# A fused chunk-attention and gated-MLP kernel on one core: the first w_in piece cast in halves, the last w_out piece and the h3 loads exchanged, the last block's small loads begun a block later

## The chip, the cores and the metric

One core of one Trainium2 chip. The metric is the device time of one execution in microseconds. Before the change: 295.74 us, median of 3 runs (294.94 to 296.02). A timed execution lasts about 1.7 us longer than the span that the profile of the same execution shows, from the first to the last instruction. The execution that was profiled for this "before" took 296.49 us, 0.75 more than the median.

## The reference

```python
# q, k, v: 8 x 8 x 576 x 64, float32; softmax attention inside chunks of 64
scores = (1 / sqrt(64)) * q_c @ k_c.transpose(0, 1, 2, 4, 3)
attn = exp(scores - max); attn = attn / (sum(attn) + 1e-9)
x = (attn @ v_c).transpose(...).reshape(4608, 512)
h = x @ w_in                                  # 512 x 2048
g = h * (1 / (1 + exp(-beta * h)))
out = g @ w_out                               # 2048 x 512
```

The kernel works on 9 blocks of 512 rows of x. Block n has two halves of attention, h = 2n and 2n + 1, so "h5" is the second half of block 2. For each half come, in order: loads of k, q, v; casts to bf16 (POOL); a transpose of q and k (for h2 to h5 on DVE, from h6 by DMA followed by an ordering copy on POOL); scores (PE); exp (ACT); averages (PE); normalising to xn (DVE); a transpose of xn to xT (on PE at first, from block 3 by DMA). Then mm1 (x by w_in, 64 matmuls per block), the gate g (ACT and DVE) and mm2 (g by w_out, 64 matmuls).

## The kernel before

The program declares operations with a rank, and a small scheduler in the kernel file turns them into **one fixed, in-order queue per engine** before the kernel is built. A change of one rank or load can therefore move instructions on several engines. These are the parts that the change touches:

```python
def cast_w_in(j, c0, c1, eng):                 # piece j of w_in, 512 columns
    s, f0, n = PIECES[j]
    stage, names = stage_w_in(j)
    cast(eng, n * (c1 - c0), w_in_bf[:, c0:c1, f0:f0 + n], stage[:, c0:c1, :],
         keys(names, ("in", j)), [K("w_in", j, c) for c in range(c0, c1)])
...
ORDER = (("w", 0), ("w", 1), ("h", 2), ("w", 2))   # loads after w_in: w_out pieces, halves
LATER = (("h", 3), ("w", 3))
...
def load_half(h, after=None):
    load(load_qk, h, 1, "sp", after=after)         # k, then q, then v in two parts
    first = load(load_qk, h, 0, "sp", after=after)
    for cp in range(2):
        load(load_v, h, cp, "sp", after=after)
    return first
...
for j in range(4):
    for c, eng in enumerate(("pool", "act", "pool", "dve" if j else "act")):
        go(0, cast_w_in, j, c, c + 1, eng)
...
for h in (2, 3):
    attention(h)
load_half(4)
load_half(5)
...
for blk in range(2, NB):                           # cut
    for i in range(16):
        go(r, mm1, blk, i, n)
        done = gated[blk, i] = go(0, gate, blk, i, n)
        if 2 <= blk < 7:                           # 24 small loads of the last block
            for fn, args, kw in small[3 * (16 * (blk - 2) + i) // 10:3 * (16 * (blk - 2) + i + 1) // 10]:
                go(5000, fn, *args, "sp", after=done, **kw)
        go(r + 2, mm2, blk - 1, s, range(p, p + w), m)
```

The softmax here doesn't subtract the row's maximum and nothing guards it: scores larger than these inputs give would overflow.

Of the kernel before, what the change touches and what calls it, by code (L numbers as in the profile page):

```python
# [12 lines left out]
def K(*key, v=0):  # L13

    return key, v
# [276 lines left out]
def bass_chunk_attention__then__act_swish_beta_kernel(nc, q, k, v, w_in, w_out, beta, out):  # L292
# [7 lines left out]
    with ExitStack() as es:  # L300
        def sb(name, shape, t):
            return es.enter_context(nc.sbuf_tensor(name, shape, t))

        P = Program(nc, es, 64)
# [4 lines left out]
        w_in_bf = sb("w_in_bf", [128, NC, DFF], BF16)  # L309
# [20 lines left out]
        A0, A1, A2, A3, F3, F0, F1, F2 = range(8)  # L330
        FS = (F0, F1, F2, F3)

        def bank(n):
            return A[:, n, :]

        def act_us(n):
            return 0.186 + 0.833e-3 * n
# [4 lines left out]
        def pool_us(n):  # L342
            return 0.07 + 1.02e-3 * n

        def copy(eng, us, dst, src, reads, writes, **kw):
            if eng == "act":
                P.op("act", us, lambda e: e.activation(dst, src, AF.Copy, **kw), reads, writes)  # L347
            else:
                P.op(eng, us, lambda e: e.tensor_copy(dst, src), reads, writes)  # L349

        def cast(eng, n, *args):
            us = {"act": act_us(n), "dve": 0.12 + 0.56e-3 * n, "pool": pool_us(n)}[eng]
            copy(eng, us, *args)
# [40 lines left out]
        def keys(names, v):  # L394
            return [K(*n, v=v) for n in names]
# [48 lines left out]
        def stage_w_in(j):  # L444
            s, f0, n = PIECES[j]
            return wstage[:, s, :].rearrange("p (c f) -> p c f", c=4), \
                [("wst", s, x, c, hb) for x in range(2) for c in range(4) for hb in range(2)]
# [5 lines left out]
                stage, w_in[:, f0:f0 + n].rearrange("(c p) f -> p c f", p=128)),  # L453
                writes=keys(names, ("in", j)))

        def cast_w_in(j, c0, c1, eng):
            s, f0, n = PIECES[j]
            stage, names = stage_w_in(j)
            cast(eng, n * (c1 - c0), w_in_bf[:, c0:c1, f0:f0 + n], stage[:, c0:c1, :],
                 keys(names, ("in", j)), [K("w_in", j, c) for c in range(c0, c1)])  # L460

        def stage_w_out(j):
            if j < 2:
# [225 lines left out]
        def piece_of(t):  # L689
            return t // 4  # L690

        def mm1(blk, t, n, halves=(0, 1)):
            sx = blk % 2
            m, j = divmod(t, 2)
            hs, c = slice(halves[0], halves[-1] + 1), slice(256 * halves[0], 256 * halves[-1] + 256)
            for kt in range(4):
                def f(e, kt=kt):
                    u, y = divmod(kt, 2)
                    return e.matmul(  # L699
                        bank(n)[:, c].rearrange("p (x t) -> p x t", t=64),  # L700
                        w_in_bf[:, kt, 256 * m:256 * m + 256].rearrange("p (x t) -> p t x", t=2)[:, j, :],
                        xT[:, sx, hs, :, :, u, 64 * y:64 * y + 64].rearrange("p v k c t -> p (v k c) t"),
                        start=(kt == 0), stop=(kt == 3))
                P.op("pe", 0.108 * len(halves), f, reads=[K("w_in", piece_of(t), kt)]
                     + [K("xT", sx, hv, y, v=2 * blk + hv) for hv in halves for y in range(2)],
                     writes=[K("ps", n, v=("h", blk, t))])

# [51 lines left out]
        def go(rank, fn, *args, slack=0, line=False, after=None, **kw):  # L759
            P.call += 1  # L760
            P.rank, P.slack, P.line, P.after, P.name = rank, slack, line, after, (fn.__name__,) + args
            fn(*args, **kw)
            P.after = None
            return P.ops[-1]
# [2 lines left out]
        FIRST = 10  # L767
        TURNED, XTURNED = 6, 6
        SL = 1.5
        TD = {2: -2, 3: 0}  # L770
        ALONE = (4, 5)
        go(-9, make_identity)
        go(-9, make_ones)
        loads = [0]
        gated = {}
        ORDER = (("w", 0), ("w", 1), ("h", 2), ("w", 2))
        LATER = (("h", 3), ("w", 3))
        URGE = {1: -1, 4: 2, 5: 2}
        TA, TB = -4, 4

        def load(fn, *args, after=None):
            loads[0] += 1
            return go(loads[0], fn, *args, line=after is None, after=after)

        def load_half(h, after=None):
            load(load_qk, h, 1, "sp", after=after)
            first = load(load_qk, h, 0, "sp", after=after)
            for cp in range(2):
                load(load_v, h, cp, "sp", after=after)
            return first  # L790

        def rank_of(h):
            return -1000 + 10 * h

        def turn(h, banks=None):
            r = rank_of(h)
            for w in (1, 0):
                if h >= 2:
                    go(r, cast_rows, h, w, "pool")
                    for hb in range(2):  # L800
                        go(TD.get(h, 2), turn_dve, h, w, hb)
                    continue
                for j in range(2):
                    go(URGE.get(h, 0), cast_qk, h, w, j, 4, ("dve", "act")[j] if h == 0 else ("dve", "pool")[j])
                for j in range(2):
                    go(r, turn_pe, h, w, j, 4, banks[2 * w + j])
                for j in range(2):
                    go(URGE.get(h, 0), keep_turned, h, w, j, 4, banks[2 * w + j],
                       "act" if h == 1 and w == 0 else ("dve", "act")[j])
            for cp in range(2):  # L810
                go(r + 1, cast_v, h, cp, "pool")

        def score(h, sb=A0):
            go(rank_of(h), *((scores, h, (0, 1), sb) if h < 2 else (scores_halved, h)))
            for cp in range(2):
                go(URGE.get(h, 0), *((exp, h, (cp,), sb) if h < 2 else (exp_halved, h, cp)))

        def average(h, banks=(A2, A0)):
            r = rank_of(h)
# [9 lines left out]
        def group(h):  # L829
            x = waiting.pop(0) if waiting and (h is None or waiting[0] <= h - 2) else None  # L830
            go(-3, turn_group, h, x, slack=0.7)

        def attention(h):
# [4 lines left out]
            else:  # L838
# [7 lines left out]
                if h < FIRST + 1:  # L846
                    go(r, scores, h, (0, 1), slack=SL)
                else:
                    go(r, attend_and_score, h - 1, slack=SL)
                    go(0, normalize_all, h - 1)  # L850
# [4 lines left out]
            elif h < FIRST:  # L855
                go(r, attend, h, (0, 1), slack=SL)
                for cp in range(2):
# [5 lines left out]
        first = load_half(0)  # L863
# [13 lines left out]
        score(1, F0)  # L877
        average(1)
        for what in ORDER:
            load(load_w_out, what[1], "sp") if what[0] == "w" else load_half(what[1])  # L880
        go(0, turn_beta, F2)
        for i in range(NWARM[2]):
            go(1e6, warm, F3, 64)
        for j in range(4):
            for c, eng in enumerate(("pool", "act", "pool", "dve" if j else "act")):
                go(0, cast_w_in, j, c, c + 1, eng)
        for t in range(4):
            go(10 * t, mm1, 0, t, FS[t], (0,))
# [6 lines left out]
        for j in range(3):  # L895
            for i in range(4):
                go(0, cast_w_out, j, i, ("pool", "dve")[i % 2])
        for what in LATER:
            load(load_w_out, what[1], "sp") if what[0] == "w" else load_half(what[1])
        for i in range(4):  # L900
            go(0, cast_w_out, 3, i, ("pool", "dve")[i % 2])
        for h in (2, 3):
# [27 lines left out]
        small = []  # L930
# [3 lines left out]
        for blk in range(2, NB):  # L934
            if blk < LAST:
                for h in (2 * blk + 2, 2 * blk + 3):
                    if blk + 1 < LAST:
                        load_half(h, after=gated[divmod(16 * (blk - 1) + (TA, TB)[h % 2], 16)])
                    attention(h)
            else:  # L940
                while waiting:
                    group(None)
                go(-500, attend_all, 2 * LAST + 1, slack=SL)
                go(0, normalize_all, 2 * LAST + 1)
                waiting.append(2 * LAST + 1)
                group(None)
            for i in range(16):
                n = FS[i % 2]
                r = 100 * blk + 400 + 4 * i
                go(r, mm1, blk, i, n)  # L950
                done = gated[blk, i] = go(0, gate, blk, i, n)
                if 2 <= blk < 7:
                    for fn, args, kw in small[3 * (16 * (blk - 2) + i) // 10:3 * (16 * (blk - 2) + i + 1) // 10]:
                        go(5000, fn, *args, "sp", after=done, **kw)
                w = 4
                s, p = divmod(w * i, 16)
                m = FS[2 + s % 2] if 2 * blk + 2 < FIRST else F2
                go(r + 2, mm2, blk - 1, s, range(p, p + w), m)
                if p + w == 16:
                    finish(blk - 1, s, m)  # L960
# [4 lines left out]
        for j in range(2):  # L965
            cols, n = (256 * j, 256 * j + 256), (F3, F0)[j]
# [56 lines left out]
```

## Time and profile before

| | before |
|---|---|
| timed | 295.74 us (3 runs) |
| span of the profiled execution | 294.8 us |
| PE busy | 280.0 us (95%) |
| DVE, ACT, POOL busy | 147.8, 147.8, 114.8 us |

PE is the bound, so the useful view is the list of what PE waited for. These are its rows of the kernel before that lie after the first 20 us; the columns are the releaser, the total in us, the number of times, the longest:

```profile
PE A L699 <- issue: 1.5, 1, 1.5
PE A L563 <- POOL qkO L349: 0.9, 1, 0.9
PE A L583 <- DVE xT L349: 0.5, 1, 0.5
PE A L699 <- DVE g L717: 0.2, 1, 0.2
```

L699 is mm1, L563 and L583 are scores. In order of time they stand at 47.6 (0.5), 57.8 (0.2, behind the gates g of block 1), 79.7 (0.9) and 105.3 us (1.5, block 3's first mm1). The last of these places is **block 3's start at about 104**.

### The profile page before, as it was taken

How to read it: one execution, taken by the hardware profiler on the slowest of the kernel's cores; microseconds unless marked ns; L12 is line 12 of the kernel's file. 1: busy time of each engine (PE TensorE's matmuls, PEld its weight loads, DVE VectorE, ACT ScalarE, POOL GpSimd, SP SyncE). 2: the span in 40 equal slices, each digit the busy share in tenths (PEclk: the TensorE clock that was granted, in tenths of full speed). 3: DMA queues.
4: the chain of work that ended last, by engine and by line, in shares of the span. 5: the costliest groups of instructions: out<-in, count | busy, mean ns of one | idle time of the engine just before them, and what ended most of it. 6: DMA issues, size and time to landing. Idle time of an engine off the chain costs nothing.

```text
span 294.8 us, 6064 instructions
## 1 busy us (share of the span) xinstructions
PE 280.0 (95%) x2584; PEld 137.6 (47%) x2584; DVE 147.8 (50%) x268; ACT 147.8 (50%) x224; POOL 114.8 (39%) x117
## 2 busy tenths in 40 slices
PE   2879998999899979999999999999999999999995
PEld 2655444644444434444444444444444444444444
DVE  2547967897356435436363636363635544334300
ACT  4548713675546525545455555555545445454311
POOL 1534655535776564554545657504350000000000
PEclk9989999999999999999999999999999999999999
DMA  7999999999989999999999898828282310101133
GB/s 202 307 389 400 285 334 313 316 260 242 217 221 205 212 284 188 295 177 254 176 271 185 262 204 227 128 89 143 91 127 98 64 71 0 73 0 71 51 88 77
DMA packets 91722, 55.97 MB, mean 190 GB/s; under 512 B 76712, under 2 KB 76976, under 8 KB 91696
## 3 DMA queue, kind: packets, MB, share of 16 engines
q1 hardware_dynamic: 91520, 55.46, 76.0%
q8 instruction: 20, 0.33, 0.4%
q10 hardware_dynamic: 176, 0.14, 0.2%
q14 instruction: 6, 0.05, 0.1%
HBM read 36.71 MB, written 9.44 MB: 157 GB/s over the span
## 4 chain that ended last, share of the span: by engine, by line
PE 81%; DMA 10%; SPq 3%; DVE 2%; POOL 2%; issue 1%; POOLq 0%
PE A L727 40%; PE A L699 38%; DMA wstage<-in_moe_w_in_dram 3%; DMA qkT<-qkb 3%; SPq L417 2%; DMA qkstage<-in_k_dram 2%; DMA qkstage<-in_q_dram 2%; PE A L612 2%; PE A L563 1%; POOL qkO L349 1%; DVE g L717 1%; SPq L432 1%; DVE qkO L521 0%; POOL w_in_bf L349 0%; DVE w_out_bf L349 0%
## 5 line engine op out<-in xcount | busy, mean ns | idle before, releaser
L717 DVE SCALAR_TENSOR_TENSOR g<-tt,A 128x512 bf16<-128x512 bf16 x144 | 97.7, 685 | 99.5 <-ACT tt L714 98.4
L699 PE MATMUL A<-xT,w_in_bf 128*128 128x512 bf16 (+1 forms) x608 | 142.1, 371 | 2.9 <-issue 1.5
L714 ACT ACTIVATE tt<-A,beta_half 128x512 bf16<-128x512 f32 x144 | 98.1, 688 | 90.2 <-PE A L699 89.9
L727 PE MATMUL A<-w_out_bf,g 128*128 128x512 bf16 (+1 forms) x592 | 140.0, 374 | 0.2
L699 PEld LDWEIGHTS A<-xT,w_in_bf 128*128 128x128 bf16 x608 | 57.9, 99 | 66.4 <-DVE g L717 6.1
L727 PEld LDWEIGHTS A<-w_out_bf,g 128*128 128x128 bf16 x592 | 56.6, 98 | 65.0 <-POOL w_out_bf L349 0.8
L349 POOL COPY qkO<-qkT 128x1024 bf16<-128x1024 bf16 x24 | 47.2, 1977 | 36.3 <-DMA qkT<-qkb 36.3
L349 POOL CAST qkb<-qkstage 128x1024 bf16<-128x1024 f32 (+1 forms) x30 | 30.7, 1025 | 23.8 <-DMA qkstage<-in_k_dram 12.7
L347 ACT ACTIVATE ostage<-A 128x512 f32<-128x512 f32 (+1 forms) x36 | 21.3, 591 | 17.6 <-PE A L727 17.6
L652 DVE TENSOR_TENSOR xn<-A,R 128x512 bf16<-128x512 f32 (+2 forms) x44 | 25.4, 592 | 1.2
L349 POOL CAST v_bf<-vstage 128x512 bf16<-128x512 f32 x32 | 19.7, 616 | 16.2 <-DMA vstage<-in_v_dram 15.8
L600 ACT ACTIVATE E<-A 128x1024 bf16<-128x1024 f32 (+1 forms) x16 | 14.4, 915 | 10.3 <-PE A L612 8.1
L657 DVE RECIPROCAL R<-A 128x8 f32<-128x8 f32 (+2 forms) x36 | 7.2, 199 | 12.5 <-PE A L612 12.5
L521 DVE STREAM_TRANSPOSE qkO<-qkb 128x256 uint32<-128x256 uint32 x16 | 9.3, 650 | 4.0 <-POOL qkb L349 4.0
L612 PEld LDWEIGHTS A<-v_bf,E 64*64 64x64 bf16 x576 | 6.9, 107 | 7.1 <-issue 4.2
L612 PE MATMUL A<-v_bf,E 64*64 64x65 bf16 x576 | 9.8, 195 | 0.0
L502 PE MATMUL A<-ident,qkb 128*128 128x128 bf16 x32 | 3.5, 267 | 6.4 <-DVE qkb L349 6.3
L592 ACT ACTIVATE E<-A 128x512 bf16<-128x512 f32 x8 | 4.5, 596 | 8.0 <-PE A L583 8.0
L349 POOL CAST w_in_bf<-wstage 128x512 bf16<-128x512 f32 x8 | 4.9, 640 | 7.8 <-DMA wstage<-in_moe_w_in_dram 7.8
L349 POOL CAST qkb<-wstage 128x1024 bf16<-128x1024 f32 x4 | 4.2, 1043 | 9.5 <-issue 9.5
L563 PE MATMUL A<-qkO 64*64 64x64 bf16 x448 | 6.6, 198 | 0.9 <-POOL qkO L349 0.9
L741 DVE TENSOR_SCALAR ostage<-A 128x256 f32<-128x256 f32 x1 | 0.4, 425 | 13.3 <-PE A L727 13.3
(35 smaller groups left out, 65.1 us busy)
## 6 DMA issues: line engine op xcount, KB each, us to landing
qkstage<-in_k_dram SPq DMA_DIRECT2D x16, 512.0 KB, 5.1
qkstage<-in_q_dram SPq DMA_DIRECT2D x16, 512.0 KB, 5.6
vstage<-in_v_dram SPq DMA_DIRECT2D x32, 256.0 KB, 6.4
out_dram<-ostage SPq DMA_DIRECT2D x16, 512.0 KB, 4.1
wstage<-in_moe_w_in_dram SPq DMA_DIRECT2D x4, 1024.0 KB, 9.9
qkstage<-in_moe_w_out_dram SPq DMA_DIRECT2D x2, 1024.0 KB, 14.8
g<-in_moe_w_out_dram SPq DMA_DIRECT2D x2, 1024.0 KB, 8.9
wstage<-in_q_dram SPq DMA_DIRECT2D x8, 128.0 KB
```

The costliest lines, as they stand in the source:

```text
L347: P.op("act", us, lambda e: e.activation(dst, src, AF.Copy, **kw), reads, writes)
L349: P.op(eng, us, lambda e: e.tensor_copy(dst, src), reads, writes)
L521: P.op("dve", 0.1 + 2.05e-3 * 256, lambda e: e.transpose(dst, qkb[:, s, which, 4 * hb:4 * hb + 4, :].rearrange("p a x -> p (a x)").bitcast ...
L563: return e.matmul(bank(b + hb)[64 * c2:64 * c2 + 64, 64 * i:64 * i + 64], qkO[r, s, 1, hp, 64 * c:64 * c + 64], qkO[r, s, 0, hp, 64 * c:64 ...
L600: P.op("act", act_us(128 * (b - a)), lambda e: e.activation(E[:, s, :, a:b, :].rearrange("p g i q -> p g (i q)"), S[:, :, 64 * a:64 * b], ...
L612: return e.matmul(bank(n)[64 * y:64 * y + 64, 65 * j:65 * j + 65], E[r, s, hb, 4 * cp + hp, :], v_bf[r, sv, 2 * hv + cp, 2 * hp + hb, 0:65])
L652: P.op("dve", 0.15 + 1.05e-3 * n, lambda e: e.tensor_tensor(dst, o[..., 0:64], r.unsqueeze(len(r.shape)).to_broadcast(shape), ALU.mult), r ...
L657: P.op("dve", 0.22, lambda e: e.reciprocal(r, o[..., 64]), reads=[K("ps", b, v=("o", h)) for b in banks], writes=[K("R", banks[0], v=h)])
L699: return e.matmul(bank(n)[:, c].rearrange("p (x t) -> p x t", t=64), w_in_bf[:, kt, 256 * m:256 * m + 256].rearrange("p (x t) -> p t x", t ...
L714: P.op("act", 0.075 + act_us(N), lambda e: e.activation(tt[:, T % 3, c], bank(n)[:, c], AF.Tanh, scale=beta_half[:, t:t + 1]), reads=[K("p ...
L717: P.op("dve", dve_us(N), lambda e: e.scalar_tensor_tensor(g2[:, sg, t, c], tt[:, T % 3, c], 1.0, bank(n)[:, c], ALU.add, ALU.mult), reads= ...
L727: P.op("pe", 0.2158 * (b - a) / 512, lambda e, t=t: e.matmul(bank(n)[:, 0:b - a], g2[:, sg, t, rows], w_out_bf[:, t, a:b], start=(t == 0), ...
```

## The change

Three parts. (1) The first w_in piece is cast in eight half casts on POOL, ACT and DVE, so that mm1 can start on a half. (2) The last two loads of the LATER list change places. The one-line description says "h3 loaded ahead of the last w_out piece"; the code does the reverse: the last w_out piece now goes ahead of h3. (3) The 24 small loads for the last block begin in block 3 instead of block 2. The diff without its settings that change nothing (they spell out what was implicit before); left out, too, is the line in which mm1 now names the half of the w_in piece that it reads:

```diff
-        def cast_w_in(j, c0, c1, eng):
+        def cast_w_in(j, c0, c1, eng, xs=(0, 1)):
...
+            a, b = 256 * xs[0], 256 * xs[-1] + 256
+            cast(eng, (b - a) * (c1 - c0), w_in_bf[:, c0:c1, f0 + a:f0 + b], stage[:, c0:c1, a:b],
+                 keys(names, ("in", j)), [K("w_in", j, c, x) for c in range(c0, c1) for x in xs])
...
+        SMALL = 3
+        FIRST_CASTS = (("pool", "act", "dve", "pool"), ("act", "pool", "act", "pool"))
...
-        LATER = (("h", 3), ("w", 3))
+        LATER = (("w", 3), ("qv", 3))
...
-        for j in range(4):
-            for c, eng in enumerate(("pool", "act", "pool", "dve" if j else "act")):
+        for x in range(2):
+            for c, eng in enumerate(FIRST_CASTS[x]):
+                go(-3, cast_w_in, 0, c, c + 1, eng, (x,))
+        for j in range(1, 4):
+            for c, eng in enumerate(("pool", "act", "pool", "dve")):
                 go(0, cast_w_in, j, c, c + 1, eng)
...
-                if 2 <= blk < 7:
-                    for fn, args, kw in small[3 * (16 * (blk - 2) + i) // 10:3 * (16 * (blk - 2) + i + 1) // 10]:
+                if SMALL <= blk < 7:
+                    y = 24 / (16 * (7 - SMALL))
+                    for fn, args, kw in small[int(y * (16 * (blk - SMALL) + i)):int(y * (16 * (blk - SMALL) + i + 1))]:
```

More of the change, by code (lines that the diff above doesn't have):

```diff
@@ L454, in load_w_in @@
                 writes=keys(names, ("in", j)))
-        def cast_w_in(j, c0, c1, eng):
+        def cast_w_in(j, c0, c1, eng, xs=(0, 1)):
             s, f0, n = PIECES[j]
             stage, names = stage_w_in(j)
-            cast(eng, n * (c1 - c0), w_in_bf[:, c0:c1, f0:f0 + n], stage[:, c0:c1, :],
-                 keys(names, ("in", j)), [K("w_in", j, c) for c in range(c0, c1)])
+            a, b = 256 * xs[0], 256 * xs[-1] + 256
+            cast(eng, (b - a) * (c1 - c0), w_in_bf[:, c0:c1, f0 + a:f0 + b], stage[:, c0:c1, a:b],
+                 keys(names, ("in", j)), [K("w_in", j, c, x) for c in range(c0, c1) for x in xs])
         def stage_w_out(j):
@@ L703, in f @@
                         start=(kt == 0), stop=(kt == 3))
-                P.op("pe", 0.108 * len(halves), f, reads=[K("w_in", piece_of(t), kt)]
+                P.op("pe", 0.108 * len(halves), f, reads=[K("w_in", piece_of(t), kt, t // 2 % 2)]
                      + [K("xT", sx, hv, y, v=2 * blk + hv) for hv in halves for y in range(2)],
@@ L769, in bass_chunk_attention__then__act_swish_beta_kernel @@
         SL = 1.5
+        SMALL = 3
+        FIRST_CASTS = (("pool", "act", "dve", "pool"), ("act", "pool", "act", "pool"))
+        PAIRED = (2, 3, 4, 5)
         TD = {2: -2, 3: 0}
@@ L775, in bass_chunk_attention__then__act_swish_beta_kernel @@
         gated = {}
-        ORDER = (("w", 0), ("w", 1), ("h", 2), ("w", 2))
-        LATER = (("h", 3), ("w", 3))
+        ORDER = (("w", 0), ("w", 1), ("qv", 2), ("w", 2))
+        LATER = (("w", 3), ("qv", 3))
         URGE = {1: -1, 4: 2, 5: 2}
@@ L783, in load, with load_half, load_what, turn @@
             return go(loads[0], fn, *args, line=after is None, after=after)
-        def load_half(h, after=None):
-            load(load_qk, h, 1, "sp", after=after)
-            first = load(load_qk, h, 0, "sp", after=after)
-            for cp in range(2):
-                load(load_v, h, cp, "sp", after=after)
-            return first
+        def load_half(h, after=None, parts="qv"):
+            if "q" in parts:
+                load(load_qk, h, 1, "sp", after=after)
+                first = load(load_qk, h, 0, "sp", after=after)
+            if "v" in parts:
+                for cp in range(2):
+                    load(load_v, h, cp, "sp", after=after)
+            return first if "q" in parts else None
+        def load_what(what):
+            if what[0] == "w":
+                load(load_w_out, what[1], "sp")
+            else:
+                load_half(what[1], parts=what[0])
         def rank_of(h):
             return -1000 + 10 * h
-        def turn(h, banks=None):
+        def turn(h, banks=(A0, A1)):
             r = rank_of(h)
             for w in (1, 0):
+                if h >= 2 and h not in PAIRED:
+                    go(r, cast_qk, h, w, 0, 8, "pool")
+                    go(r, turn_pe, h, w, 0, 8, banks[w])
+                    go(URGE.get(h, 0), keep_turned, h, w, 0, 8, banks[w], ("act", "dve")[w])
+                    continue
                 if h >= 2:
@@ L813, in score @@
         def score(h, sb=A0):
-            go(rank_of(h), *((scores, h, (0, 1), sb) if h < 2 else (scores_halved, h)))
+            go(rank_of(h), *((scores_halved, h) if h in PAIRED else (scores, h, (0, 1), sb)))
             for cp in range(2):
-                go(URGE.get(h, 0), *((exp, h, (cp,), sb) if h < 2 else (exp_halved, h, cp)))
+                go(URGE.get(h, 0), *((exp_halved, h, cp) if h in PAIRED else (exp, h, (cp,), sb)))
         def average(h, banks=(A2, A0)):
@@ L879, in bass_chunk_attention__then__act_swish_beta_kernel @@
         for what in ORDER:
-            load(load_w_out, what[1], "sp") if what[0] == "w" else load_half(what[1])
+            load_what(what)
         go(0, turn_beta, F2)
@@ L898, in bass_chunk_attention__then__act_swish_beta_kernel @@
         for what in LATER:
-            load(load_w_out, what[1], "sp") if what[0] == "w" else load_half(what[1])
+            load_what(what)
         for i in range(4):
```

## The prediction

> **What bounds the kernel now.** I read the page first, then the chain that ended last, then the timeline of the places where TensorE (PE) pauses. The page's opening rows:
>
> ```profile
> span 294.8 us, 6064 instructions
> PE 280.0 (95%) x2584; PEld 137.6 (47%) x2584; DVE 147.8 (50%) x268; ACT 147.8 (50%) x224; POOL 114.8 (39%) x117
> PE   2879998999899979999999999999999999999995
> DMA  7999999999989999999999898828282310101133
> ```
>
> PE is the bound: 280.0 of 294.8 us busy, so only 14.8 us of idle exist. The third row says where: the first two slices (7.4 us each), the last one, and digits below 9 around slices 5, 10 and 14. Nothing else on PE changes with this diff: it runs the same 2584 matmuls. The last row says that the DMA engines are full for nearly the first half, which decides below who keeps a gain.
>
> The chain of waits, in order of time, shows what PE hung on in the middle:
>
> ```profile
> 50.01 5.33 DMA qkstage<-in_q_dram
> 55.47 1.05 POOL qkb L349
> ...
> 61.17 5.50 DMA qkstage<-in_k_dram
> 66.67 9.09 DMA qkT<-qkb
> 75.81 3.88 POOL qkO L349 x2
> ...
> 103.80 1.50 issue
> ```
>
> So from 50 to 79.7 us the path runs through loads, a DMA transpose (9.09 us) and two POOL copies, not through PE. PE has work beside it until 78.83 and then waits 0.91 us (row L563 <- POOL qkO). At 103.80 it waits again, 1.50 us. From 105.31 us to the end the chain is PE back to back, so the finish is the moment PE passes 105.31 plus a constant 189.5 us (294.8 - 105.31). This is my main lever: **a saving counts only if it moves that moment.**
>
> The timeline of the two ends of the region:
>
> ```profile
> 18.13 1.15 ACT L347 ACTIVATE w_in_bf<-wstage 128x512 bf16<-128x512 f32 x2 [1.75 <-DMA wstage<-in_moe_w_in_dram]
> 18.16 1.18 POOL L349 CAST w_in_bf<-wstage 128x512 bf16<-128x512 f32 x2 [3.43 <-DMA wstage<-in_moe_w_in_dram]
> 18.83 0.39 PE L699 MATMUL A<-xT,w_in_bf 128*128 128x256 bf16 x2 [0.99 <-POOL w_in_bf L349]
> 19.39 0.91 PE L699 MATMUL A<-xT,w_in_bf 128*128 128x256 bf16 x6 [0.17 <-POOL w_in_bf L349]
> ...
> 95.77 1.57 SPq L423 DMA_DIRECT2D wstage<-in_q_dram  x2
> 97.45 2.75 SPq L539 DMA_TRANSPOSE qkT<-qkb  x2
> 100.25 1.63 SPq L539 DMA_TRANSPOSE xT<-xn  x1
> ...
> 105.31 1.02 PE L699 MATMUL A<-xT,w_in_bf 128*128 128x512 bf16 x4 [1.50 <-issue]
> ```
>
> The upper four: the first w_in piece lands at about 18.13, its four casts run two by two on ACT and POOL until about 19.34, and PE waits for them (0.99 + 0.17 us). The lower four: the xT transpose that block 3's first matmul needs is issued at 100.25. Transposes of xT take 3.1 to 4.9 us (median 4.3) from issue to landing, so 103.4 to 105.2, which fits the matmul's start at 105.31. The "issue" label names no releaser; xT is my reading. Ahead of it in the queue stand two small loads for the last block (1.57 us), and one more at 82.62.
>
> [...] granted clock 0.50 from 20.0 to 23.4, full after; 3.4 us at half rate costs about 1.7 us of matmul time. [...] POOL casts of 512 columns take 616 ns alone and 838 ns where DVE casts at the same moment, whose own time goes from 421 to 631. [...] In this trace the small load at 82.62 held the SP queue 2.6 us for a wait.
>
> **Part 1, casts in halves.** A POOL cast goes from 616 ns to about 0.33 us and an ACT cast from 629 ns to about 0.42 ([...] estimates from these rows); a DVE cast from 421 to about 0.28. Before: first weight ready 18.78, fourth 19.34. After: POOL c0 18.16 to 18.5, ACT c1 to 18.55, DVE c2 [...] to 18.4–18.8, POOL c3 to about 18.85–19.1. The second halves are done at 19.5–19.8. PE starts about 0.3 us earlier, can do 12 matmuls before the last transposes of x instead of 8, and begins the second-half matmuls at about 21.05 instead of 22.2. Of these 16, 11 run at half clock until 23.4 (2.35 us / 0.213) and 5 at full (0.54), ending near 23.95; before, 6 and 10, ending near 24.5. **Gain at this point: 0.55 us.** A cost is hidden in the order: DVE's cast stands between its two normalisations, so the second waits for the landing and xn is ready at 19.3–19.7 instead of 18.22. That meets PE, which only comes to those transposes at about 19.9. [...]
>
> **Part 2, load order.** The description speaks of h3 before the last w_out piece; the code does the reverse. The last w_out piece (1 MB) now goes right behind the third, h3 after it. That piece landed at 47.5 and PE was waiting around it: 0.52 us at 47.12 and the weight loads 0.63 at 49.2. Now it lands near 42.2 (1 MB at about 0.3 MB/us behind 38.8). h3's q lands about 3.5 us later, 45.5 instead of 42.0; cast 1.04 and two DVE transposes 1.3 put its scores at about 47.9–48.2. PE's new order puts 8 more w_out matmuls (8 x 0.216 = 1.73 us) ahead of those scores, so it comes there at 47.12 + 1.73 - 0.55 = 48.3. It just fits. **Gain: the 0.5 us of idle, with up to 0.5 at risk.**
>
> **Together at block 1:** PE is about 1.0 us early at 55. But it then meets the DMA-bound stretch. SP issues without a pause there, and the bytes ahead of h6's q are the same in both kernels. So the qkT landing at 75.76 and PE's restart at 79.74 stay, and the wait of 0.91 grows to about 1.9. **Parts 1 and 2 are given back at 79.7**, except what the altered order of the two output stores moves in the queue: I allow +0.3 us, within -0.5 to +1.
>
> **Part 3, small loads from block 3.** Three of them leave the queue ahead of the xT transpose that is late at 105. SP saves 95.77 to 97.45, 1.65 us. If only the data's time is saved, 2 x 128 KB at 309 GB/s is 0.85 us. So xT lands 0.85 to 1.65 us earlier, 103.6 to 104.4, while PE comes at 103.80 as before. The wait of 1.50 shrinks to between 0 and 0.65: **gain 0.85 to 1.5, middle 1.2.** Later blocks take 6 small loads instead of 4.8, but the running total (6 after block 3 against 9.6, 12 against 14.4, 18 against 19.2, 24 against 24) never exceeds the old one, and PE has no idle there. I charge nothing.
>
> **Sum:** 0 from parts 1 and 2 directly, 0.3 from the altered queue, 1.2 from part 3 = 1.5 us, so 295.74 - 1.5 = 294.2.
>
> **Rivals.** (a) The gains add up, because the DMA stretch moves with PE: 0.55 + 0.5 + 0.9 + 1.5 = 3.4 us, 292.3. For it: the stretch contains gates by DVE g at 57–61, which follow PE. Against it: SP is issuing without a gap until 66.6. (b) The late h3 becomes the new wait at 48, half a microsecond or one. For it: h3's margin is under 0.4 us. Against its mattering: there is 0.9 + 0.55 us of slack before 79.7. It would leave 294.2, and only a slip beyond 1.5 us would show. (c) The xT transpose is late because of the DMA engines (busy share 1.1 to 1.19 from 100 to 106), not the SP queue; then part 3 returns only 0.4 and the time is 295.3. (d) Another order in the queue delays h6 and costs 1 us: 295.5.
>
> **Range and chances.** The middle is 294.2. Rival (a) and an escape from the half clock reach to 292.6, (c) and (d) to 295.5; the old runs alone spread over 1.1 us. I take 292.7 to 295.4. Being 2% faster needs 5.9 us, more than all middle idle and the half clock together (0.55 + 1.35 + 0.5 + 0.9 + 1.5 = 4.8): 3%. Slower by 2% would need a new 6 us stall in a stream of unchanged totals: 1%.
>
> **What would show it.** Right: first w_in matmul near 18.5; the wait near 47 gone; PE's wait before the scores at 79–80 grown to about 1.9 with the restart still near 79.7; the wait near 104 under 0.7; PE solid after that. Wrong: the restart at 79.7 moving earlier with PE (then the sum is too small); a wait of over 1.5 us at h3's scores; the 104 wait unchanged; idle appearing in blocks 3 to 7, where small loads are denser.

The forecast's sum is 0 + 0.3 + 1.2 = 1.5 us, so 294.2. One term outside the sum, a gain of 1.9 us at the head if PE is not at half clock there, stands as 0.55 + 1.35 under "Range and chances", as a possibility for which no trace shows what brings it about. The times of the half casts are estimates; in the look at the change one took 427 ns on POOL, 405 on ACT and 294 on DVE on average, against 616, 629 and 421 for a whole one in the text above.

## The result

295.38 us (median of 6 runs, 294.67 to 296.48) against 295.78 (6 runs, 294.94 to 296.38) of the kernel before beside it. The ratio is 0.999, with a 95% interval of 0.9966 to 1.0015: the same within 2%. Ratios here are the mean time of one kernel's fast runs over the mean of the other's of the same rounds, so not quite the ratio of the medians that are quoted. The forecast was 1.5 us of gain; 0.4 was measured.

The page of the kernel after:

```profile
span 293.7 us, 6073 instructions
PE 278.3 (95%) x2584; PEld 136.7 (47%) x2584; DVE 147.6 (50%) x269; ACT 148.0 (50%) x225; POOL 115.9 (39%) x119
```

What PE waited for after, in the same view as before (L700 is mm1, L584 is scores; every line number has moved by one):

```profile
PE A L700 <- DVE g L718: 2.2, 1, 2.2
PE A L584 <- DVE xT L349: 0.9, 1, 0.9
PE A L700 <- DMA xT<-xn: 0.8, 1, 0.8
```

The wait for POOL at 79.7 is gone, and the wait at block 3 shrank from 1.5 to 0.8. But the wait for the gates at 58 grew from 0.2 to 2.2 us. The head, from the timeline (start, length, engine, operation, and in brackets the idle time before it and its releaser):

```profile
17.99 1.03 ACT L347 ACTIVATE w_in_bf<-wstage 128x256 bf16<-128x256 f32 x3 [1.68 <-DMA wstage<-in_moe_w_in_dram]
17.99 0.29 DVE L349 CAST w_in_bf<-wstage 128x256 bf16<-128x256 f32 x1 [0.67 <-DMA wstage<-in_moe_w_in_dram]
18.02 1.55 POOL L349 CAST w_in_bf<-wstage 128x256 bf16<-128x256 f32 x4 [3.32 <-DMA wstage<-in_moe_w_in_dram]
18.60 1.50 PE L700 MATMUL A<-xT,w_in_bf 128*128 128x256 bf16 x12 [0.82 <-POOL w_in_bf L349]
```

Part 1 works as meant: PE starts at 18.60 and does 12 matmuls at once, where before it did 2 at 18.83 and 6 more at 19.39. In this execution PE also kept its full clock (granted clock 1.00 from 14 to 26 us). It came to h3's scores at 47.43 without a wait, with eight more mm2 matmuls (1.73 us) done than before at 47.64, so 1.9 us early, and to h4's 1.5 early. After 16 more mm1 matmuls it stood still for 2.18 us, until 58.25. Before and after, from PE's timeline:

```profile
55.01 0.71 PE L583 MATMUL A<-qkO 32*64 32x64 bf16 x64
57.78 1.90 PE L699 MATMUL A<-xT,w_in_bf 128*128 128x512 bf16 x8 [0.21 <-DVE g L717]
```

```profile
53.50 0.71 PE L584 MATMUL A<-qkO 32*64 32x64 bf16 x64 [0.85 <-DVE xT L349]
58.25 1.90 PE L700 MATMUL A<-xT,w_in_bf 128*128 128x512 bf16 x8 [2.18 <-DVE g L718]
```

The 0.85 us before h4's scores is a new wait too, for a copy of xT that stands behind two transposes of h4 in DVE's queue. The chain of waits says what the 2.18 us were for (start, length, step):

```profile
48.33 1.05 POOL qkb L349
49.41 1.15 DVE qkO L522 x2
50.61 5.21 DMA qkstage<-in_q_dram
55.94 1.05 POOL qkb L349
58.25 1.90 PE A L700 x8
...
96.51 1.72 SPq L540
98.27 4.86 DMA xT<-xn
103.26 1.89 PE A L700 x8
```

And DVE's timeline just before 58:

```profile
55.70 1.15 DVE L522 STREAM_TRANSPOSE qkO<-qkb 128x256 uint32<-128x256 uint32 x2 [2.25 <-POOL qkb L349]
57.01 0.66 DVE L522 STREAM_TRANSPOSE qkO<-qkb 128x256 uint32<-128x256 uint32 x1 [0.17 <-POOL qkb L349]
57.51 0.68 DVE L718 SCALAR_TENSOR_TENSOR g<-tt,A 128x512 bf16<-128x512 bf16 x1
```

In DVE's in-order queue the first three gates of block 1 stand behind three transposes of h5. Two of these wait for POOL's cast of h5's k, the third for its cast of h5's q, and that waits for h5's q to land. The gates' own inputs, three operations on ACT, were done between 55.5 and 56.6. PE needs the first gate because the gate reads a buffer of A that PE's next matmuls write (so the kernel declares it; the timeline names DVE's g as the releaser of the 2.18 us). So however early PE is, it cannot pass 58 before h5's q has landed (50.61 + 5.21 us), and that load was issued at 50.01 before and 50.61 after.

### The profile page after: what moved, and what is told of

The parts are those of the page before. It is cut to its first block, busy times and chain, and to the rows that moved or that the text cites. A ratio compares the mean times of both kernels' runs of the same rounds, so it can differ in the third digit from the quotient of the medians.

```text
span 293.7 us, 6073 instructions
## 1 busy us (share of the span) xinstructions
PE 278.3 (95%) x2584; PEld 136.7 (47%) x2584; DVE 147.6 (50%) x269; ACT 148.0 (50%) x225; POOL 115.9 (39%) x119
## 4 chain that ended last, share of the span: by engine, by line
PE 77%; DMA 12%; SPq 8%; DVE 1%; POOL 1%; issue 0%; ACT 0%; POOLq 0%
PE A L728 37%; PE A L700 36%; SPq L432 4%; DMA wstage<-in_moe_w_in_dram 3%; DMA qkstage<-in_k_dram 3%; DMA g<-in_moe_w_out_dram 2%; PE A L613 2%; DMA qkstage<-in_q_dram 2%; SPq L417 2%; DMA xT<-xn 2%; PE A L564 1%; SPq L473 1%; SPq L540 1%; POOL qkb L349 1%; DVE qkO L522 1%
## 5 line engine op out<-in xcount | busy, mean ns | idle before, releaser
L700 PE MATMUL A<-xT,w_in_bf 128*128 128x512 bf16 (+1 forms) x608 | 140.7, 368 | 3.9 <-DVE g L718 2.2
L700 PEld LDWEIGHTS A<-xT,w_in_bf 128*128 128x128 bf16 x608 | 57.3, 98 | 67.7 <-DVE g L718 8.4
L349 POOL CAST w_in_bf<-wstage 128x512 bf16<-128x512 f32 (+1 forms) x10 | 5.7, 600 | 7.0 <-DMA wstage<-in_moe_w_in_dram 7.0
L347 ACT ACTIVATE xT<-A 128x512 bf16<-128x512 bf16 x6 | 3.6, 593 | 8.0 <-PE A L679 8.0
```

Of the source, the lines that this page charges most:

```text
L347: P.op("act", us, lambda e: e.activation(dst, src, AF.Copy, **kw), reads, writes)
L349: P.op(eng, us, lambda e: e.tensor_copy(dst, src), reads, writes)
L700: return e.matmul(bank(n)[:, c].rearrange("p (x t) -> p x t", t=64), w_in_bf[:, kt, 256 * m:256 * m + 256].rearrange("p (x t) -> p t x", t ...
```

## The experiments

Eighteen runs, all with 5 rounds: a profile, and 6 runs against 10 to 12 of the kernel before on the same chip. Runs of one call ran on one chip and share the runs of before (chip 3 for e1 to e8, chip 4 for e9 to e18). Two numbers of each profiled execution (called a look below) are used throughout: the moment PE passes the gates (the start of the mm1 group that waits at 58) and the wait at block 3's first mm1. The third is their check: **span minus the gates' moment minus the later waits is 234.3 to 234.6 us in all but three of the executions read** (e3, where PE's order is another; e7, see there; e8, where the clock fell). So in the others PE is solid from 58 on but for the waits listed, and these places decide.

| run | kernel | median us | ratio, 95% | gates: moment, wait | block 3 wait | span |
|---|---|---|---|---|---|---|
| before | - | 295.78 | - | 57.78, 0.21 | 1.50 (and 0.91 at 79) | 294.8 |
| after | all three | 295.38 | 0.999 (0.9966-1.0015) | 58.25, 2.18 | 0.83 | 293.7 |
| e1 | before again | 295.93 | 1.0003 (0.9982-1.0024) | 58.82, 0.19 | 0.89 | 294.2 |
| e2 | part 1 | 296.25 | 1.001 (0.9988-1.0033) | 58.23, 0.29 | 1.67 | 294.4 |
| e3 | part 2 | 296.56 | 1.0035 (1.0-1.0071) | 60.07, 1.28 | 1.74 | 297.0 |
| e4 | part 3 | 294.68 | 0.9953 (0.9933-0.9974) | 57.73, 0.24 | 0 | 292.1 |
| e5 | all three | 295.71 | 0.9949 (0.9906-0.9992) | 58.86, 1.09 | 0 | 293.2 |
| e6 | 1 + 3 | 294.64 | 0.9923 (0.9883-0.9962) | 58.79, 0.89 | 0 | 293.1 |
| e7 | all, gates first | 295.03 | 0.9934 (0.9891-0.9977) | 58.72, 0.19; 62.45, 0.49 | 0 | 294.1 |
| e8 | all, four ahead | 296.85 | 0.998 (0.9931-1.0029) | 58.61, 2.16 | 0 (0.26 later) | 295.1 |
| e9 | all three | 295.04 | 0.9969 (0.9943-0.9995) | 58.47, 1.87 | 1.02 | 294.0 |
| e10 | part 3 | 295.01 | 0.9963 (0.9937-0.9989) | 59.46, 0.19 | 0 | 293.8 |
| e11 | all, half load | 293.6 | 0.9936 (0.9901-0.9972) | 56.12, 0.41 | 0.84 | 291.5 |
| e12 | part 3, half load | 294.56 | 0.9945 (0.9915-0.9975) | 59.26, 0.19 | 0 | 293.6 |
| e13 | all, q first | 294.74 | 0.9957 (0.9925-0.9988) | 57.84, 0.19 | 0.97 | 293.3 |
| e14 | 1 + 3, q first | 296.35 | 1.0003 (0.9968-1.0037) | 57.47, 0.30 | 0 | 291.8 |
| e15 | 1 + 3 | 294.7 | 0.9951 (0.9923-0.9979) | 58.03, 0.53 | 0 | 292.4 |
| e16 | all three | 295.65 | 0.9996 (0.9959-1.0033) | 58.38, 1.92 | 1.03 | 293.9 |
| e17 | all, xT ahead | 294.51 | 0.9952 (0.992-0.9984) | 58.16, 1.28 | 0 | 292.5 |
| e18 | all, xT ahead, q first | 293.7 | 0.9928 (0.9901-0.9955) | 57.43, 0.19 | 0 | 291.8 |

The calls were e1 to e4, e5 to e8, e9 to e12, e13 to e16, and e17 with e18. In the second call two runs of the kernel before took 298.54 and 299.95, so its ratios flatter every kernel; there the medians are the better measure.

### The parts alone (e1 to e4)

**e1_same_again**: the kernel before, unaltered.

> The kernel before, byte for byte, as a control and for a second profile. Theory A (the one profile that I read overstated the waits): the ratio is 1.000 within 0.3%, and the second profile shows a wait before block 3's first matmul near 104 us clearly below the 1.50 us of the first, or a restart after the scores of h6 away from 79.7 us by over 0.3 us. Theory B (the waits are fixed and the changed kernel lost elsewhere): the second profile repeats 0.91 and 1.50 us within 0.2.

**e2_casts_only**: part 1 of the diff alone.

> Only the halved casts of the first w_in piece. Theory A (what is saved before 58 us is given back where the loads of h5 or the transposes of h6 arrive): PE early by 0.5 to 2 us at 35 us, but the time within 0.3 us of before (-0.3 to +0.3). Rival (gains add): 0.5 us faster[...].

**e3_order_only**: one line.

```diff
-        LATER = (("h", 3), ("w", 3))
+        LATER = (("w", 3), ("h", 3))
```

> Only the last w_out piece ahead of h3. Theory A: the wait of 0.5 us near 47 goes, and a longer one shows near 57 (gates queued on VectorE behind h5's transposes); time within 0.3 us of before. Rival C (this part costs what another part gains, through the later h3, h4, h5 loads): 0.4 to 1.0 us slower.

**e4_small_only**: part 3 alone.

> Only the small loads a block later. Theory A: the transpose of xT before block 3 is issued about 1.6 us earlier, the wait near 104 falls below 0.7 us and the time by 0.4 to 0.8 us, as much as that wait is in a typical run. Rival C (the parts cancel): 1.0 to 1.5 us faster, and another part loses it. Rival D (the transpose engine work, not the queue, is late): no change, under 0.2 us.

Measured in medians against 296.05 of before: the copy -0.1, casts +0.2, order +0.5, small loads -1.4 us. Part 3 gives about what the prediction gave it (1.2), the size of rival C and not of A (0.4 to 0.8), and in its profile the wait at block 3 is gone. Part 1 gives nothing, as A said. Part 2 alone rather costs, as rival C said, but its two slowest runs, 298.5 and 298.7, carry the mean, and the slower of them is its look. The copy shows how much one look can differ: its waits at 79 and at block 3 were 0 and 0.89 where the first profile of the same program had 0.91 and 1.50. The 1.5 us on which the prediction's third part was sized came from one execution, and the second look did not repeat it.

### Do the parts cancel? (e5, e6, e15, e16)

**e5_change_again** and **e16_change_fourth**: the changed kernel, nothing altered. **e6_casts_and_small** and **e15_casts_and_small_again**: the changed kernel with LATER as before.

> The changed kernel once more, nothing altered, on the chip and in the rounds of the next three. Theory A (the parts cancel: the small loads give 0.47% back, the load order takes about 0.35% of it): ratio to the kernel before 0.998 to 1.000. Rival R1 (nothing cancels, the first measurement of the changed kernel was unlucky and its true gain is that of the small loads): ratio 0.994 to 0.996. A also expects the same three signs in the profile: a wait of about 2 us behind the gates near 58, PE at block 3's first matmul near 102.5 and a wait for xT of 0.5 to 1.2 us there.

> Parts 1 and 3 without the load order. Theory A: the load order is what eats the gain, so the gain of the small loads stays: ratio 0.994 to 0.996, no wait at block 3, the wait behind the gates near 58 under 0.6 us. Rival R2 (the halved casts eat it, because PE then arrives early and meets every later wait): ratio 0.998 to 1.000, and a wait of over 1 us near 58.

> Parts 1 and 3 again, to settle whether part 2 costs 1.1 us, as in the first call that had both, or nothing, as the comparison of the change with part 3 alone said. If it costs (theory A as first stated): 0.6 to 1.2 us below the changed kernel of this call. If that was chance (R1): within 0.4 us of it.

> The changed kernel as the reference of this call. Theory A: PE passes the gates at 58.2 to 58.9, xT's wait at block 3 either 0 or 0.8 to 1.0 us; 295.0 to 295.7 us. If part 2 costs: 0.6 to 1.2 us above parts 1 and 3 of this call; if not, within 0.4 us.

Without part 2 the kernel ended 1.07 us earlier in one call (294.64 against 295.71) and 0.95 in the other (294.70 against 295.65). Both are inside the 0.6 to 1.2 us that e16 and e15 had for a part 2 that costs. Rival R1, that the first measurement of the change was merely unlucky, is right only in part: e5's ratio (0.9949) fell in R1's range and its look lacks the wait at block 3 that A expected, but the change's own ratio spread from 0.9949 to 0.9996. The spans of the looks of e5 and e6 are alike (293.2 and 293.1), so that call shows its loss in the timed runs alone. Rival R2, that the casts eat the gain, falls: with the casts and part 3 together the gain is all there.

The static order says that from block 1 on **no queue differs** between the two kernels except in the places of a few loads and stores. So what part 2 costs is hardly a matter of order from there on; when loads and stores move and land is left. In the looks one thing stands out: the wait at block 3. Three of the four looks at the changed kernel have it (0.83, 1.02, 1.03; e5 has none), and with part 3 in and part 2 out no look has it (e4, e6, e10, e12, e14, e15).

### Which place holds the gates at 58? (e7, e11, e12, e13, e14)

**e7_change_gates_first**: in DVE's finished queue the three gates are moved ahead of h5's transposes (`move`, a helper that the run defines, is left out).

```diff
         P.schedule()
+        move("dve", [("gate", 1, t) for t in range(3)], ("turn_dve", 5))
         P.build()
```

> The changed kernel with one queue altered: on VectorE the first three gates of block 1 stand ahead of the four stream transposes of h5 instead of behind three of them; every other queue is the same. Theory A says that the 2.18 us wait at 58 is these gates standing behind a transpose whose load is late, and that it sets everything up to block 3 about 0.5 us later: the wait should fall under 0.5 us, PE should reach block 3 about 0.5 us or more earlier and the time fall by 0.4 to 1.0 us against the changed kernel of the same call. Rival R3 (from 58 on the path runs through the loads, PE's wait there costs nothing): the wait at 58 goes, another of about the same length appears by 80 or at block 3, and the time stays within 0.2 us of the changed kernel.

The median fell by 0.68 us against e5, inside A's range, but the look is against A: the wait at 58 went (0.19), another came at 62.45 (0.49), and h5's scores started 0.8 us later than in e5 (70.22 against 69.40), as R3 had it. This look was also the slowest of its kernel's 6 runs: the half clock at the head lasted from 18.4 to 25.0 us in it, against 19.3 to 22.7 in e5, so PE came later to everything. e7 alone decides nothing.

**e11_change_half_load** and **e12_small_half_load**: half the bytes of the last w_out piece, in the changed kernel and in the kernel with part 3 alone. Their outputs are wrong, which doesn't matter for the times.

```diff
+            ms = slice(0, 1 if j == 3 else 2)
             P.dma(queue, (0.65, 16, 149), lambda e: e.dma_start(
-                stage.rearrange("p (m x) -> p m x", m=2),
-                w_out[512 * j:512 * (j + 1), :].rearrange("(m p t) d -> p m (t d)", m=2, t=2)),
+                stage.rearrange("p (m x) -> p m x", m=2)[:, ms, :],
+                w_out[512 * j:512 * (j + 1), :].rearrange("(m p t) d -> p m (t d)", m=2, t=2)[:, ms, :]),
...
```

The cut part lets the two casts of the missing half take the loaded half again.

> The changed kernel a third time, as the reference for the run with half the load, and as one more execution to read. Theory A (PE comes to the gates of block 1 early and waits for the loads; the end is the moment PE passes there plus 234.3 us plus any wait at block 3): the wait ends between 58.2 and 58.9, and span minus that moment minus the wait at block 3 is within 0.2 of 234.4. Time 295.2 to 295.8 us.

> Part 3 alone again, as the reference of the same call. Theory A: no wait at block 3, PE passes the gates of block 1 between 57.6 and 58.3, a wait under 0.4 us there; time 0.5 to 1.0 us below the changed kernel of this call. Rival R1 (the difference between the two is chance): within 0.3 us of it.

> The changed kernel with half the bytes of the last w_out piece (0.5 MB, about 1.7 us of the loads' time at 0.31 MB/us); its two unloaded casts take the loaded half again, so the result is wrong on purpose, and every queue keeps its order. Theory A (parts 1 and 2 bring PE to the gates 1 to 2 us early and the loads ahead of h5's q hide it): the wait at 58 falls under 0.6 us, PE passes there at 57.3 or earlier, and the time falls by 0.8 to 1.7 us against the changed kernel of this call. Rival R4 (the loads are not what holds that place; the wait is DVE's own order or POOL's work): the moment at 58 moves by under 0.3 us and so does the time.

> The same halved load in the kernel with part 3 alone, where PE waits only 0.2 us at the gates and 0.5 us at h3's scores. Theory A: PE itself is the bound there, so the halved load gives at most the waits it meets, 0.2 to 0.8 us, clearly less than in the changed kernel. Rival R5 (both kernels hang on the loads alone, PE's place in them does not matter): the same gain as in the changed kernel, within 0.3 us. The result is wrong on purpose.

(The 0.31 MB/us of e11's expectation is an estimate; the kernel before moved 312 GB/s on average from 40 to 60 us, and the change 299.) The halved load moved the gates in the changed kernel from 58.47 to 56.12 and its time from 295.04 to 293.60: 1.4 us, as A said. PE's timeline of e11 at that place:

```profile
56.12 1.90 PE L702 MATMUL A<-xT,w_in_bf 128*128 128x512 bf16 x8 [0.41 <-DVE g L720]
```

PE was there at 55.7, and only 0.41 us of the 2 us of waiting is left. In the kernel with part 3 alone the same halving was worth 0.45 us (295.01 to 294.56), again A's side. So the loads hold the gates when parts 1 and 2 are in, and **PE's earliness from them is real and hidden**. R4 and R5 fall. (In e12's look PE was late by its own clock, at half rate from 18.5 to 25.3 us; the mean granted clock of that execution was 0.988.)

e10 missed twice: it was expected 0.5 to 1.0 us ahead of e9 and was not (295.01 against 295.04), and PE passed its gates at 59.46, not between 57.6 and 58.3. Here part 2 cost nothing. The look shows why part 2 had been wanted. This is PE waiting for the cast of the last w_out piece in e10:

```profile
48.82 1.40 PE L727 MATMUL A<-w_out_bf,g 128*128 128x512 bf16 x3 [2.43 <-DVE w_out_bf L349]
```

That wait was 2.43 us here, 1.41 in e6, 1.73 in e15, 0.51 in e14, and no look with part 2 has it at this place. In e10 the clock fell behind it as well, from 49.5 to 52.9 us (0.994 as the mean of the execution); the row of that stretch has 0.50 as the granted clock, the third number from the end:

```profile
50.00:52.00 2.00, 2.00 (x37) 0.96 (x37) 1.62 (x5) 0.60 (x1) 1.72 (x3) 0.50 0.91 167
```

Both made PE itself late at the gates (59.46, wait 0.19). That is 0.99 us later than in e9, as much as e9 lost at block 3 (1.02), so in these two looks the load order took from one place what it gave at the other. Without part 2 the gates are sometimes PE's own (57.7 to 59.5 in e4, e10 and e12), and with part 2 they are the loads' (58.2 to 58.9 in the looks at the change).

**e13_change_q_first** and **e14_no_order_q_first**: h5's k and q are loaded ahead of h4's v, in the changed kernel and in parts 1 and 3. Results are right, PE's order is the same.

```diff
-        load_half(4)
-        load_half(5)
+        for h, part in ((4, "q"), (5, "q"), (4, "v"), (5, "v")):
+            load_half(h, parts=part)
```

> The changed kernel with one thing altered: h5's k and q are loaded ahead of h4's v (0.5 MB fewer bytes ahead of h5's q, right result; PE's order is the same). Theory A (the loads hold the gates of block 1, PE is early there): like the halved load, PE passes the gates 1 us or more earlier than 58.2, wait there under 0.6 us, and the time falls by 0.8 to 1.7 us against the changed kernel of this call; but h4's averages must not wait for the later v for more than 0.3 us. Rival R6 (h4's v becomes the new wait, or what follows at 79 and block 3 hangs on the loads and comes no earlier): the time within 0.3 us of the changed kernel.

> Parts 1 and 3 without part 2, with h5's k and q ahead of h4's v in the same way. Theory A: PE comes to the gates less early than in the changed kernel (it waited 0.9 us there, and 1.4 us for the last w_out piece), so the gain against parts 1 and 3 is 0.4 to 1.0 us, less than that of the run above. If part 2 is worth its half microsecond once the loads no longer hide it, this run ends 0.3 to 0.8 us later than the run above; if part 2 is worth nothing, within 0.2 us.

e13 took 294.74 against 295.65 of e16: 0.9 us, and the wait at the gates fell to 0.19. The gates' moment came only 0.5 us earlier (57.84), less than A's 1 us, because PE met a new wait of 0.50 at 55.35. e14 missed what was expected (0.4 to 1.0 us below e15; it was 1.65 above): its look is the best of all in that call (293.53, span 291.8), but four of its six runs took 296.3 to 297.1. Between the two groups lie 1.7 us and more; why is open. A fall of the clock in mid-kernel, as in e10 and e8, is a rival that no run tested: 3.4 us at half rate (e10, 49.5 to 52.9) cost about 1.7, an estimate that takes half of that time. The mean clocks do not tell the groups apart (0.994 and 0.994 against 0.988 and three times 0.994).

### What does part 2 cost, and where? (e8, e17, e18)

**e8_change_four_ahead**: four mm2 matmuls of block 2 are moved ahead of block 3's first mm1 in PE's finished queue.

```diff
         P.schedule()
+        move("pe", [("mm2", 2, 0, range(4, 8))], ("mm1", 3, 0))
         P.build()
```

> The changed kernel with one queue altered: on PE, four w_out matmuls of block 2 (0.86 us) stand ahead of block 3's first w_in matmul instead of behind it, as in the kernel before; every other queue is the same. Theory A: the work left behind the wait for xT counts, so with 0.86 us of it moved ahead, the wait of 0.83 us shrinks under 0.3 us and the time falls by 0.5 to 0.9 us against the changed kernel of the same call. Rival R3: the wait stays near 0.8 us because xT comes later by as much, and the time stays within 0.2 us.

Both sides missed: the wait at block 3 went, and the time rose by 1.1 us against e5. The table of stretches of that look suggests why (the number before the DMA share and the GB/s is PE's granted clock):

```profile
54.00:58.00 4.00, 2.44 (x80) 1.96 (x76) 1.77 (x4) 2.86 (x5) 2.08 (x2) 1.00 1.12 328
58.00:60.00 2.00, 1.39 (x6) 0.66 (x7) 2.00 (x5) 0.94 (x2) 0.96 (x2) 0.92 0.96 282
60.00:62.00 2.00, 2.00 (x36) 0.80 (x35) 1.41 (x3) 1.12 (x2) 0.27 (x1) 0.50 0.95 298
62.00:64.00 2.00, 2.00 (x8) 0.84 (x7) 1.50 (x3) 0.49 (x1) 1.04 (x1) 0.73 1.12 316
```

After the idle of 0.81 and 2.16 us PE fell to half clock from about 59.7 to 63.1, where nothing hides it any more: the stretch from the gates to the end took 236.2 us instead of 234.3 to 234.6. The six runs fit: the two with a mean clock of 0.999 and 1.0 took 295.35 and 295.12, the other four (0.988 to 0.994) 296.8 to 297.2, though a mean does not say where the clock fell. That the waits caused the fall was not shown. In the unaltered change no look has the fall: after, e9 and e16 had nearly the same two waits (0.85 to 0.89 and 1.87 to 2.18) and kept the full clock (0.998 to 1.0 as the mean of the execution).

**e17_change_xT_ahead**: in SP's finished queue the transpose of h7's xn goes ahead of h9's two transposes. **e18_xT_ahead_q_first**: that and e13's edit.

```diff
         P.schedule()
+        q = P.queues["sp"]
+        i = [n for n, o in enumerate(q) if o.get("unit") and o["unit"]["name"] == ("turn_group", 9, 7)]
+        assert len(i) == 3 and i[2] == i[0] + 2, i
+        q.insert(i[0], q.pop(i[2]))
         P.build()
```

> The changed kernel with one queue altered: in SP's queue the transpose of h7's x (whose input is ready at 94.2) stands ahead of h9's two transposes instead of behind them, so it is issued near 95 instead of 98.3; every other queue is the same. Theory B (what the load order takes from the small loads' gain is the wait for xT at block 3: 0.83, 0, 1.02 and 1.03 us in the four looks at the changed kernel, 0 in five looks without the load order): no wait at block 3, PE passing the gates near 58.4 as before, and a time 0.5 to 1.0 us below the changed kernel's, that is a ratio to the kernel before of 0.994 to 0.997 where the four calls gave 0.995 to 1.000 (mean 0.9976). Rival R7 (the loss comes from elsewhere, for example from executions in which PE passes the gates later): the wait goes and the time stays at a ratio of 0.9976 within 0.001.

> Both repairs on the changed kernel: h7's transpose of x ahead of h9's, and h5's k and q ahead of h4's v. Theory B with A: PE passes the gates near 57.8 (0.5 us before the changed kernel) and has no wait at block 3 (0.97 us in the run with q first alone), so 0.4 to 0.8 us below the run above of this call and a ratio to the kernel before of 0.991 to 0.994: the best of all kernels here. Rival R6 (something after the gates, at 79 or block 3, takes the place): within 0.3 us of the run above.

SP's queue in the changed kernel, and then in e17 (start, length of the issue):

```profile
94.97 3.25 SPq L540 DMA_TRANSPOSE qkT<-qkb  x2
98.27 1.35 SPq L540 DMA_TRANSPOSE xT<-xn  x1
```

```profile
95.10 1.53 SPq L540 DMA_TRANSPOSE xT<-xn  x1
96.67 2.96 SPq L540 DMA_TRANSPOSE qkT<-qkb  x2
```

xT is issued 3.2 us earlier, and block 3 starts without a wait:

```profile
102.17 1.89 PE L700 MATMUL A<-xT,w_in_bf 128*128 128x512 bf16 x8
```

e17 took 294.51 us, ratio 0.9952, where the four measurements of the unaltered change gave 0.9976 on average: 0.7 us, the size of the wait's mean over its four looks ((0.83 + 0 + 1.02 + 1.03) / 4 = 0.72). R7 is not supported, but it is not excluded either: e17's interval (0.992 to 0.9984) still holds 0.9976, and no run of the unaltered change shared its call. e18 is the best kernel: 293.70 us, 2.6 below the kernel before of its call (296.32), ratio 0.9928 (0.9901 to 0.9955), with the gates at 57.43 (wait 0.19) and no wait at block 3.

## Why the prediction was wrong

**The bound and the lever: right.** PE is solid to the end after block 3's first matmul, and head gains count only if they move that moment. The constant 189.5 us behind it was 189.46 in e1 and 189.45 in e2. It is not a constant of the change: the new order leaves four more mm2 matmuls behind that point (0.86 us), and 293.7 - 103.26 gives 190.44. The order of the queues, which could be seen before the prediction, shows it; e4 has it and e2 has not, so it comes with part 3.

**Part 1, gain at the head and none at the end: right in outcome.** PE starts at 18.60 (18.5 was expected), and e2 ended 0.2 us later than before, not earlier. The half clock at the head lasted 3.4 us (20.0 to 23.4) in the first look at the kernel before and 10.2 us (14.2 to 24.4) in e1's look at the same program. The escape from it, which the prediction counted at 1.9 us (0.55 + 1.35) and set beside rival (a), happened in three of the four looks at the change (all but e5), and the spans were 293.7, 294.0 and 293.9 against 293.2 for e5, where the clock was at half from 19.3 to 22.7. So even an escape from about 1.7 us of loss at the head (an estimate: half of those 3.4 us) does not arrive. What brings the escape about was not shown.

**Where parts 1 and 2 are given back: the right mechanism, the wrong place.** The prediction put it at h6's scores: "the wait of 0.91 grows to about 1.9" at 79.7. In the change that wait is 0, and the 2.2 us stand at 58, behind the gates and h5's q. I had read the row "57.78 ... 0.21 <-DVE g" as following PE, and did not follow those gates back through DVE's queue to the transposes ahead of them. e11 and e13 show the load behind it.

**Part 2, "it just fits": right.** The waits near 47 and 49 are gone, and h3's later loads made no new one (rival b): PE came at 47.43 and did not wait. Of its 1.9 us it lost about 0.4 net by h4's scores, at the new wait of 0.85 that the prediction did not have.

**Part 3: right.** Predicted 1.2 us; alone it gave 1.4 and 1.1 (e4, e10), and the wait at block 3 is 0 in both looks.

**The term that failed is "0.3 from the altered queue", together with "PE comes at 103.80 as before".** The prediction gave the new order +0.3 us (within -0.5 to +1). Beside parts 1 and 3 the order costs 1.07 and 0.95 us in the two calls that had both. That takes most of part 3's gain: of 1.5 predicted, 0.7 are left on average over four calls (1 - 0.9976, of 296). PE came at 102.4 and not at 103.8: the wait of 0.91 at 79 was gone and four mm2 matmuls (0.86) had moved behind this point, against gates that were 0.47 later. It then met xT, whose issue had moved from 100.25 to 98.27 and which took 4.86 us to land. For xT the prediction was not too hopeful (103.6 to 104.4 expected, the matmul started at 103.26); it did not ask how early PE would be. e17 takes that wait away, and its ratio is lower by 0.7 us, within the limits said there.

**What stays open.** Why xT lands 4.9 to 5.1 us after its issue in the looks that wait, and within 4.1 to 4.4 in e4 to e7, e14 and e15, where PE came then and did not wait. The queues there are nearly the same. So the step from part 2 to the late xT is seen in the looks and not explained. Why e14's runs fall in two groups is open as well. The 1.0 us rests on the medians of two calls; the third, e9 against e10, compared the change with part 3 alone and found nothing.

**The forecast also leaned on one execution.** Its "before" had the waits 0.91 and 1.50; the copy had 0 and 0.89. That execution took 296.49 us, and the gain read from it was taken from a median of 295.74. What did come true of parts 1 and 2, that nothing of them reaches the end, was in part luck: it held at another place than the one named.

**Slips in the working.** PE's row has its digits below 9 in the middle in slices 7, 11 and 15, not "around slices 5, 10 and 14". Rival (a) alone makes 292.3, below the 292.6 to which it is said to reach together with an escape from the half clock. The casts' 838 and 631 ns are means: single casts of w_out took 801 to 875 ns on POOL and 420 to 841 on DVE, so some DVE casts were not slowed at all.

## What to carry to other kernels

Follow each wait of the bounding engine not only to its releaser but through the releaser's in-order queue: here PE waited (2.18 us in the look at the change) for a gate whose input from ACT was ready at about 55.5 us, but which stood until 57.51 behind a transpose that waited for a load. When you make the bounding engine earlier ahead of a stretch that the loads set, look for the first place where it meets them, and move that load or that queue entry instead; with e18's two small reorderings the change gave 2.1 us (by the ratio), against 0.7 alone in other calls. And look at two or three executions before sizing a gain from a wait of one microsecond.
